# Nyström attention and a SiLU MLP on one core: a written-out order, a compact Newton-Schulz iteration, and C v by single heads

## The chip, the core and the metric

The kernel runs on one core of a Trainium2 chip. A core has five engines with a queue of instructions each: TensorE (PE: matmuls, with a second row PEld for its weight loads), VectorE (DVE), ScalarE (ACT), GpSimd (POOL) and SyncE (SP). An engine takes its instructions in the order in which they were issued, and an instruction that waits for a semaphore holds up all that stand behind it. 16 DMA engines move data; in this kernel POOL issues the loads that change type on the way (fp32 to bf16 or fp16), SP the transposes and most stores. The metric is the device time of one execution in microseconds, the lower the better. A profile is taken of one execution; its span goes from the first to the last instruction.

## The reference

Eight batches, eight heads, 576 positions, head size 64. Each sequence is cut into 32 segments; the means of q and k over a segment are the landmarks.

```python
q_lm = q.reshape(B, H, m, S // m, D).mean(axis=3)     # m = 32
k_lm = k.reshape(B, H, m, S // m, D).mean(axis=3)
A  = sm(q, k_lm)          # 576 x 32, softmax of scale * a b^T
Bm = sm(q_lm, k_lm)       # 32 x 32
C  = sm(q_lm, k)          # 32 x 576
Z = Bm.T / (norm1(Bm) * norminf(Bm) + 1e-06)
for _ in range(6):
    Z = 2 * Z - Z @ Bm @ Z                            # Newton-Schulz
attn = A @ Z @ C @ v
x = attn.transpose(0, 2, 1, 3).reshape(4608, 512)
h = x @ w_in                                          # 512 x 2048
out = (h * sigmoid(h)) @ w_out                        # 2048 x 512
```

All inputs and the output are fp32 in HBM.

## The kernel before

**Stages of a batch** (`attn(b)`). The eight heads are two groups (`g`) of four; four heads of 32 landmarks fill 128 partitions. q and k are loaded as bf16 (`load_qk`, names `ld1.b` for k, `ld0.b` for q; batch 0 in four parts, `ld10 ld11 ld00 ld01`) and v in three parts (`ldv0..2`). They are turned into `qT` by TensorE transposes for batches 0 to 2 (`tr`, copied out by `trc`) and by DMA transposes issued on SP from batch 3 on (`xt`, line 592). Landmarks come from TensorE sums (`lms`) or VectorE trees (`lra` to `lrd`, line 628), and are transposed by `ltr`. `sb` makes the 32x32 scores, `pb` to `bmx` their softmax, `A` and `C` the two wide score matrices, with exponentials `Ax` and `Cx` on ScalarE, row sums `S` on TensorE and `Ln`, `Rs`, `etn` to normalise A. C is transposed by TensorE for batches 0 and 1 (`ctm`) and by DMA after that (`ct`, line 856). `cv` multiplies it by v, `zt` joins C v and Z, and `m` folds that into w_in: M = Z C v w_in, so that layer 1 is A M.

**Newton-Schulz.** The state `st` of a group is 128 x 160: a block-diagonal 128x128 matrix of four heads (F = Z Bm) and, beside it, the four Z as 128x32 (`SW = 128 + L`). Iteration `ns` multiplies the 128x128 part by all 160 columns, and `nsd` (line 754, VectorE) forms 2 s - product. `f0` and line 736 make the first state; the last iteration does the 32 columns of Z alone.

**The MLP.** Layer 1 (`h0` to `h15` of a batch, `hx` for leftover columns) is A M in 128x512 PSUM banks, `g` and `gx` are the SiLU on ScalarE into fp16. Layer 2 works on pairs of 128-row tiles with seven products instead of eight (`p1` to `p7`, sums `ss` on VectorE, results `c..`, `u2` copied or added into `ost`, stores `os`); the first pair alone is done plainly (`o0` to `o3`, names `o0@5000.0` and so on, one for each quarter of `w_out`), since the sums of w_out (`wt`) are made meanwhile.

**The order.** Every step is an `Op` with its engine, its dependencies and a priority. `Plan.run` walks through a modelled time, takes on each engine the ready step with the lowest priority, and gives it PSUM banks (bank 7 and two others serve layer 2). It shifts priorities by the table `ORDER`, and where TensorE would stand idle in the first 45 us it puts in a filler, a matmul on zeros (`warm`, tile `zer`). A load may be issued when the load eight before it has landed (`swdge[-8]`), and loads of batch 3 and later also wait for transposes (`gate` in `later_loads`). All loads are issued on POOL, in this order: k and q of batches 0 and 1, v of batch 0, w_in by four column blocks (`wi0` to `wi3`, each in three parts), w_out in four parts (`wo0` to `wo3`), v of batch 1, k and q of batch 2, v of batch 2.

Of the kernel before, what the change touches and what calls it, by code (L numbers as in the profile page):

```python
# [18 lines left out]
ORDER = {  # L19
    "f0.0": (200.69, 0), "A.0": (-135.46, 12.93), "Ln11.0": (-57.289, 0), "etn1.0": (-31.554, 0),  # L20
    "ctm00.0": (-1364.2, 0), "wc.0": (-5319.5, 0), "mc11.0": (-629.91, 0), "tr10.1": (-42.668, 0),
    "trc15.1": (-1007.6, 0), "tr19.1": (-457.92, 0), "tr114.1": (-85.703, 0),
    "tr00.1": (-4845.1, 0), "tr09.1": (-1.1208, 0), "tr014.1": (-139.96, 0),
    "lms116.1": (413.98, 0), "lms000.1": (-607.71, 0), "lms006.1": (-83.37, 0),
    "lms010.1": (328.48, 0), "nsd00.1": (-627.38, 0), "ns10.1": (2306.7, 0),
    "nsd10.1": (-1204.8, 0), "A.1": (-266.77, 0), "Ax10.1": (-230.29, 0), "Rs1.1": (-127.11, 0),
    "Cx00.1": (-281, 0), "Cx01.1": (-181.38, 0), "Cx11.1": (-2693.4, 0), "tr014.2": (-314.54, 0),
    "bbd.2": (-120.57, 0), "nsd40.2": (175.02, 0), "h15.1": (234.98, 0), "lrd1.3": (-791.6, 0),
    "A.3": (-480.16, 0), "S00.3": (52.867, 0), "Ln01.3": (24.258, 0), "Ax11.3": (-2.2697, 0),
    "h3.2": (185.78, 0), "hx0.2": (41.862, 0), "h11.2": (452.76, 0), "hx8.2": (-6.3754, 0),  # L30
    "p5@5200.0": (-179, 0), "c12@5220.0": (-251.23, 0), "A.4": (-78.982, 0),
    "etn1.4": (1667.8, 0), "Cx11.4": (29.753, 0), "cv0.4": (-3300.5, 0),
    "p6@5340.0": (-4.9303, 0), "p7@5340.0": (-4146.8, 0), "Ax10.6": (162.02, 0),
    "ss00@5500.0": (-5226.2, 0), "p7@5700.0": (633.04, 0), "p4@5720.0": (524.17, 0),
}
# [31 lines left out]
class Plan:  # L67
# [3 lines left out]
    WARM = 45.0  # L71
# [9 lines left out]
    start_warm = 1.1  # L81
    filler = None

    def run(self):
        import heapq
        order = []
        for o in self.ops:
            o.left = len(o.deps)
            shift, o.ready = ORDER.get(o.name, (0.0, 0.0))
            o.prio += shift  # L90
            for d in {id(d): d for d, _ in o.deps}.values():
                d.users.append(o)
        cand = {e: [] for e in self.LAG}
        idle = {"PE": 1.0, "ACT": 1.0, "DVE": 0.9, "POOL": 1.3, "SP": 1.0}
        banks = [0] * 8
        table = ["exp"]
        group = [None, 0]
        pending = [False]
        groups = {}
        for o in self.ops:  # L100
            if o.group is not None:
                groups[o.group] = groups.get(o.group, 0) + 1
        tiled = [None]
        dmaq = [0.0]
        events = sorted(set(idle.values()) | {o.ready for o in self.ops})
        waiting = []

        def activate(o):
            for e, _ in o.engs:
                cand[e].append(o)  # L110

        for o in self.ops:
            if not o.left:
                activate(o)

        l1_at = set()
        l1_open = {}
        l1_seen = set()
        l2_on = [False]
        l2_open = {}  # L120
        wide = [False]

        def fit(o):
            if o.cls == "L2":
                pool = (7, 6) if wide[0] else (7, 6, 5)
                if o.pair is not None and l2_open:
                    n = sum(not banks[i] for i in pool)
                    if o.pair != next(iter(l2_open)) and (o.pair in l2_open or n < 2):
                        return None
            elif o.cls == "L1":  # L130
                room = 1 if pending[0] or group[0] is not None and group[1] > 3 else 4
                if wide[0]:
                    return None
                if len(l1_at) >= room:
                    return None
                pool = (4, 3, 2, 1, 0)
            else:
                pool = (0, 1, 2, 3, 4, 5) if l2_on[0] else (0, 1, 2, 3, 4, 5, 6)
            free = [i for i in pool if not banks[i]]
            return tuple(free[:o.psum]) if len(free) >= o.psum else None  # L140

        n = 0
        total = len(self.ops)
        while n < total:
            if not events:
                raise RuntimeError("plan stuck: " + ", ".join(
                    f"{o.name}" for e in cand for o in cand[e])[:600])
            t = heapq.heappop(events)
            while events and events[0] <= t + 1e-9:
                heapq.heappop(events)  # L150
            moved = True
            while moved:
                moved = False
                for e in ("PE", "ACT", "DVE", "POOL", "SP"):
                    if idle[e] > t + 1e-9:
                        continue
                    best, bslot, later, soon = None, None, None, None
                    if e == "PE":
                        wide[0] = any(o.psum == 4 and o.ready <= t + 1e-9 and (
                            o.opens is None or group[0] == o.opens) for o in cand[e])  # L160
                    for o in cand[e]:
                        r = o.ready + o.margin
                        if r > t + 1e-9:
                            if later is None or r < later:
                                later = r
                            if o.crit and (soon is None or r < soon):
                                soon = r
                            continue
                        rank = o.prio
                        if e == "PE" and tiled[0] and o.tiled == tiled[0]:  # L170
                            rank -= 1e5
                        if best is not None and rank >= brank:
                            continue
                        if e == "ACT" and o.table == "silu" and group[0] is not None:
                            continue
                        if e == "ACT" and o.group is not None and group[0] != o.group:
                            if o.early is not None and table[0] == "exp":
                                pass
                            elif group[0] is not None or l1_open:
                                continue  # L180
                            elif o.early is not None and any(
                                    x.done is None or x.done > t + 1e-9 for x in o.early):
                                continue
                            elif len(l1_at) > 2:
                                pending[0] = True
                                continue
                        if o.opens is not None and group[0] != o.opens and (
                                group[0] is not None or l1_open or len(l1_at) > 2):
                            if group[0] is None and not l1_open:
                                pending[0] = True  # L190
                            continue
                        s = None
                        if o.psum:
                            s = fit(o)
                            if s is None:
                                continue
                        best, bslot, brank = o, s, rank
                    if best is None:
                        if later is not None:
                            heapq.heappush(events, later)  # L200
                        if e == "PE" and not banks[7] and self.start_warm <= t < self.WARM and (
                                later is None or later > t + 0.12):
                            end = t + (0.22 if t < self.start_warm + 4.4 else 0.11)
                            order.append((self.filler, e, t, end, False))
                            idle[e] = end
                            heapq.heappush(events, end)
                            tiled[0] = None
                        continue
                    o = best
                    if soon is not None and not o.crit:  # L210
                        d = max(d2 for e2, d2 in o.engs if e2 == e)
                        if t + d > soon + 0.06:
# [3 lines left out]
                    for e2, d2 in o.engs:  # L216
                        cand[e2].remove(o)
                        if e2 == e:
                            dur = d2
# [95 lines left out]
def kernel(  # L315
# [9 lines left out]
    nc = tc.nc  # L325
# [880 lines left out]
```

## Time and profile before

| what | value |
|---|---|
| three runs, us | 247.73, 249.36, 249.66 (median 249.36) |
| span of the profiled execution | 246.7 us |
| granted TensorE clock | 1.00 in every stretch |
| ScalarE busy, 0 to 40, 40 to 220, 220 to 246.7 us | 30.3, 149.3, 4.1 us |
| VectorE busy, same stretches | 24.5, 134.6, 12.6 us |
| HBM read, written | 36.7 MB, 9.4 MB |

The page shows, in its second part, 40 slices of the span with one digit each: the busy share in tenths (9 is 90% or more).

```profile
PE   8999999999979999999999999999999999999993
DVE  2368956495869956949999879189798667066632
ACT  2597996599865999998668998966988978822200
POOL 8435733200022003200220040000000000000000
DMA  5999999999999979989899799897443003022352
```

How to read the rows that follow. A group of instructions reads "line, engine, operation, output<-inputs, shape, count | busy us, mean ns of one | idle time of the engine before them <-what ended it". Matmuls are pipelined, so the mean duration of one is longer than the distance between two; the distance is read from the timeline, whose rows begin with the start and the length in us of a run of like instructions. L394 is the helper through which all matmuls but two kinds of transposes go, so its groups are told apart by tiles.

### The profile page before, as it was taken

Reading aid. Unit: us, or ns where it says so; the run is one execution under the profiler, and the core shown is the slowest. Engines: PE = TensorE matmul, PEld = TensorE weight load, DVE = VectorE, ACT = ScalarE, POOL = GpSimd, SP = SyncE. Lnnn points to the kernel's source line nnn. Section 1 sums busy time; section 2 is a strip of 40 time slices with the busy share of each in tenths; the row PEclk is TensorE's granted clock in tenths of the full one; section 3 lists DMA queues with packets and bytes.
Section 4 is the critical chain, followed back from the end, with each engine's and each line's share of the span. In section 5 each row is a group of like instructions: output and inputs, shape, how many; then the busy total and the mean of one; then the engine's idle time right before and its main releaser. Section 6 shows DMA issues by size and latency. Waiting matters only on the chain.

```text
span 246.7 us, 7075 instructions
## 1 busy us (share of the span) xinstructions
PE 238.9 (97%) x2771; PEld 170.8 (69%) x2771; DVE 171.8 (70%) x441; ACT 183.6 (74%) x438; POOL 37.2 (15%) x63
## 2 busy tenths in 40 slices
PE   8999999999979999999999999999999999999993
PEld 6786565566767645577886655697886566688883
DVE  2368956495869956949999879189798667066632
ACT  2597996599865999998668998966988978822200
POOL 8435733200022003200220040000000000000000
PEclk9999999999999999999999999999999999999999
DMA  5999999999999979989899799897443003022352
GB/s 103 203 203 193 196 208 206 207 246 166 181 115 215 208 145 152 212 135 158 168 233 229 150 170 226 146 184 99 118 119 101 0 3 85 3 73 62 82 141 72
DMA packets 55874, 36.50 MB, mean 148 GB/s; under 512 B 36641, under 2 KB 47393, under 8 KB 55841
## 3 DMA queue, kind: packets, MB, share of 16 engines
q0 software_dynamic: 15264, 18.35, 44.6%
q1 hardware_dynamic: 39808, 16.92, 33.2%
q10 hardware_dynamic: 768, 0.79, 1.3%
q8 instruction: 21, 0.34, 0.5%
q14 instruction: 13, 0.10, 0.1%
HBM read 36.70 MB, written 9.44 MB: 187 GB/s over the span
## 4 chain that ended last, share of the span: by engine, by line
PE 83%; DMA 7%; DVE 3%; ACT 3%; SPq 1%; issue 1%; POOL 0%; DVEq 0%; POOLq 0%
PE ps L394 80%; DMA qT<-qk 4%; DMA qk<-in_q_dram 3%; PE ps L568 2%; SPq L592 1%; ACT m L404 1%; DVE red L628 1%; PE ps L844 1%; DVE st L754 1%; ACT ce L829 1%; ACT L956 1%; POOL qk L447 0%; ACT ln L794 0%; DVE etn L803 0%; DVE ss L1044 0%
## 5 line engine op out<-in xcount | busy, mean ns | idle before, releaser
L394 PE MATMUL ps<-etn,m 128*128 128x512 bf16 (+1 forms) x512 | 68.9, 286 | 0.4 <-ACT gm L956 0.4
L956 ACT ACTIVATE gm<-ps 128x512 f16<-128x512 f32 x128 | 66.1, 652 | 2.0 <-PE ps L394 1.8
L394 PEld LDWEIGHTS <-gm 128*128 128x128 f16 x512 | 48.7, 98 | 11.3 <-issue 2.4
L394 PE MATMUL ps<-w_out_sb,gm 128*128 128x256 f16 (+1 forms) x392 | 53.6, 281 | 0.0
L394 PEld LDWEIGHTS <-m 128*128 128x128 bf16 x512 | 32.0, 98 | 24.0 <-issue 1.8
L404 ACT COPY ost<-ps 128x256 f32<-128x256 f32 (+1 forms) x48 | 18.4, 383 | 37.4 <-PE ps L394 30.3
L394 PEld LDWEIGHTS <-ss 128*128 128x128 f16 x408 | 39.1, 98 | 6.6 <-issue 0.9
L1079 DVE TENSOR_TENSOR ost<-ost,ps 128x256 f32<-128x256 f32 x51 | 21.2, 416 | 20.4 <-PE ps L394 14.2
L394 PE MATMUL ps<-wt,ss 128*128 128x256 f16 x272 | 34.1, 273 | 0.0
L754 DVE SCALAR_TENSOR_TENSOR st<-st,ps 128x320 bf16<-128x320 bf16 (+3 forms) x54 | 21.4, 404 | 9.0 <-PE ps L394 7.8
L406 DVE CAST m<-ps 128x512 bf16<-128x512 f32 x31 | 20.0, 683 | 0.4 <-PE ps L394 0.2
L406 DVE COPY ost<-ps 128x256 f32<-128x256 f32 x22 | 9.3, 422 | 14.9 <-PE ps L394 14.8
L404 ACT CAST m<-ps 128x512 bf16<-128x512 f32 x33 | 17.9, 601 | 1.8 <-PE ps L394 1.7
L394 PE MATMUL ps<-w_out_sb,ss 128*128 128x256 f16 x136 | 17.6, 273 | 0.0
L453 POOL DMA_DIRECT2D qk<-in_k_dram x7 | 5.0, 714 | 82.7 <-DMA ct<-ce 41.9
L460 POOL DMA_DIRECT2D v<-in_v_dram x24 | 14.0, 591 | 14.5 <-PE ps L394 6.9
L394 PE MATMUL ps<-zer 128*128 128x256 bf16 x79 | 14.7, 310 | 1.1 <-DVE zer L487 1.1
L394 PE MATMUL ps<-wt,gm 128*128 128x256 f16 x120 | 15.5, 272 | 0.0
L394 PEld LDWEIGHTS <-st 128*128 128x128 bf16 x96 | 8.4, 97 | 9.0 <-issue 2.9
L394 PE MATMUL ps<-st 128*128 128x160 bf16 (+1 forms) x96 | 14.4, 225 | 0.2 <-DVE wsb L889 0.2
L829 ACT ACTIVATE ce<-ps 128x288 bf16<-128x288 f32 x32 | 12.8, 413 | 0.0
L784 ACT ACTIVATE et<-ps 128x288 bf16<-128x288 f32 x32 | 10.6, 423 | 2.3 <-PE ps L394 2.2
(91 smaller groups left out, 331.3 us busy)
## 6 DMA issues: line engine op xcount, KB each, us to landing
out_dram<-ost SPq DMA_DIRECT2D x128, 64.0 KB, 2.1
v<-in_v_dram POOLq DMA_DIRECT2D x24, 192.0 KB, 11.2
qk<-in_k_dram POOLq DMA_DIRECT2D x7, 576.0 KB, 7.5
qk<-in_q_dram POOLq DMA_DIRECT2D x7, 576.0 KB, 10.6
w_out_sb<-in_moe_w_out_dram POOLq DMA_DIRECT2D x4, 512.0 KB, 10.4
w_in_sb<-in_moe_w_in_dram POOLq DMA_DIRECT2D x4, 256.0 KB, 9.2
w_in_sb<-in_moe_w_in_dram POOLq DMA_DIRECT2D x8, 128.0 KB, 7.9
qk<-in_k_dram POOLq DMA_DIRECT2D x2, 288.0 KB, 4.3
```

Of the source, the lines that this page charges most:

```text
L394: nc.tensor.matmul(out=out_ap, lhsT=lhsT, rhs=rhs, start=start, stop=stop, skip_group_check=True)
L404: nc.scalar.copy(out=out, in_=in_)
L406: nc.vector.tensor_copy(out=out, in_=in_)
L453: lambda e, t=t, src=src: nc.gpsimd.dma_start(out=qk_r[b % 2][:, t].rearrange("p g j d -> p g (j d)"), in_=src[b].rearrange("(g h) (l j) d ...
L460: lambda e, a=a: nc.gpsimd.dma_start(out=v_r[b % 2][a * L:(a + 1) * L, :, :], in_=v[b].rearrange("h (l a x) d -> a l h (x d)", l=L, a=VA)[ ...
L568: nc.tensor.transpose(out=ps[:, n * 128:(n + 1) * 128], in_=qk[:, t, g, 2 * jp:2 * jp + 2, :].rearrange("p j d -> p (j d)"), identity=idb)
L592: lambda e, t=t, g=g: nc.sync.dma_start_transpose(out=qT[:, t, g], in_=qk[:, t, g].rearrange("p j d -> p (j d)")),
L754: nc.vector.scalar_tensor_tensor(out=s2[:, g0:g1, lo:SW], in0=s[:, g0:g1, lo:SW], scalar=2.0, in1=ps[:, 0:NG * SW].rearrange("p (g x) -> p ...
L784: lambda e, g=g, et=et, c=c: nc.scalar.activation(out=et[:, c], in_=bank(me["A"], 2 * g + c)[:, 0:HS], func=AF.Exp, scale=sc / J),
L829: nc.scalar.activation(out=ce[:, :, 0:VP].rearrange("p (i c) (a l) -> p c a i l", c=2, a=VA)[:, c], in_=bank(me["C"], 2 * g + c)[:, 0:HS]. ...
L956: lambda e, dc=dc, cell=cell: nc.scalar.activation(out=gm[:, dc, :], in_=bank(cell["o"]), func=AF.Silu),
L1079: nc.vector.tensor_tensor(out=out_, in0=x, in1=y, op=OP.add)
```

## The change

It does five things. **The order** is no longer computed: a table, `SEQUENCE`, lists all steps in the order in which they are issued, with the engine after a slash where there is a choice, and `*n` for n fillers on TensorE; `Plan.run` reads it and hands out PSUM banks first in, first out. Fillers go from 79 to 70. In the table's POOL order the loads stand as `ld11.0 ld00.0 ld01.0 ld0.1 ld1.1`, two parts of v of batch 0, the w_in parts mixed with the third and with v of batch 1, then q and k of batch 2, then w_out, then k of batch 3 with one part of its v, and the rest.

**Newton-Schulz** holds both F and Z as 128x32 (`SW = 2 * L`). The block-diagonal matrix that TensorE needs is made from F before each iteration by a new VectorE step `fb`, a multiplication by the mask `hmask` into a tile of 128x128 a group. `f0` has 32 instead of 128 columns.

**C v** is formed head by head: 128x32 parts of the array and 64 columns, 48 matmuls a batch, where two heads at a time took 128x64 parts and 128 columns, 24 matmuls. `wc` writes the result twice with broadcast reads.

**Half of k of batch 0** (`ld10`) is loaded in fp32 by SP (`ldk`) into the space of `gm`, and cast by ScalarE (640 columns) and VectorE (512).

**v of batch 1** stands in the middle of w_in in `LOADS`. One dependency of `hx` is added.

```diff
-ORDER = {
...
+SEQUENCE = """
+ldk ld11.0 const ident fold k0cACT k0cDVE k0 *15 lms100.0 lms106.0 tr10.0 tr15.0 trc15.0/ACT
...
+ns11.0 nsd11.0 S10.0 Ln10.0 S11.0 Ln11.0 Rs1.0 trc05.1/DVE fb20.0 fb21.0 ctm00.0 ctc00.0/DVE
...
+mc10.1/ACT mc11.1/ACT *1 m2.1 lra1.2 tr014.2 trc014.2/DVE o0@5001.0 o0@5000.0 h4.1 mc20.1/ACT
...
+os3@5721.0/ACT l1done.6 l1done.7 os0@5721.0/SP os2@5721.0/SP os1@5720.0/ACT
...
     def run(self):
...
+        for word in SEQUENCE.split():
+            if word[0] == "*":
+                order += [(self.filler, "PE", 0.0, 0.0, False)] * int(word[1:])
+                continue
+            name, _, e = word.partition("/")
+            o = named.pop(name)
...
+            if o.psum:
...
+                o.slot = tuple(free[:o.psum])
+                del free[:o.psum]
...
-    SW = 128 + L
+    SW = 2 * L
...
-    LOADS = "k1 q1 v0 w0 w1 w2 w3 o0 o1 o2 o3 v1".split()
+    LOADS = "k1 q1 v0 w0 w1 v1 w2 w3 o0 o1 o2 o3".split()
...
+    def first_load():
+        o = A("ldk", [("SP", 0.45)], lambda e: nc.sync.dma_start(
+            out=stage, in_=k[0][0:4].rearrange("h (l j) d -> (h l) (j d)", l=L)), [], -300,
+            dma=1.1, lag=1.0)
+        dst = qk_r[0][:, 1, 0].rearrange("p j d -> p (j d)")
+        parts = ((0, JA * Dh, "ACT", act_us), (JA * Dh, J * Dh, "DVE", dve_us))
...
-                w = bbd[:, g].rearrange("p a l -> p (a l)")
-                mm(ps[:, g * 128:(g + 1) * 128], w, w)
+                mm(ps[:, g * L:(g + 1) * L], bbd[:, g].rearrange("p a l -> p (a l)"), bmt[:, g])
...
+            def diag(it, o, g0=g0, g1=g1, n=n):
+                return chain(f"fb{it}{g0}", 0.07 + 0.00055 * 128 * n, lambda:
+                             nc.vector.tensor_tensor(
+                                 out=fb[it % 2][:, g0:g1],
+                                 in0=bc(sr[it % 3][:, g0:g1, 0:L], 4, 2),
+                                 in1=bc(hmask, n, 1), op=OP.mult), [o], 14.5 + 0.1 * g0)
...
-                        mm(ps[:, g * SW + lo:(g + 1) * SW], s[:, g, 0:128], s[:, g, lo:SW])
+                        mm(ps[:, g * SW + lo:(g + 1) * SW],
+                           fb[it % 2][:, g].rearrange("p a l -> p (a l)"), s[:, g, lo:SW])
...
-                        for p in range(2):
-                            h = 4 * g + 2 * p
-                            hs = slice(h, h + 2) if not g else slice(h + 1, h - 1, -1)
-                            mm(wv[64 * p:64 * p + 64, g], ct_r[g][0:VP, i, 64 * p:64 * p + 64],
-                               vs[:, hs, i * Dh:(i + 1) * Dh], start=(i == 0), stop=(i == VI - 1))
+                        for h in range(4):
+                            mm(wv[L * h:L * h + L, g], ct_r[g][0:VP, i, L * h:L * h + L],
+                               vs[:, 4 * g + h, i * Dh:(i + 1) * Dh], start=(i == 0),
+                               stop=(i == VI - 1))
```

## The prediction

> **What bounds the kernel now.** I read the page first (busy shares and the chain that ended last), then the groups with their shapes, then TensorE's timeline, and for the first 50 us the DMA issues. The page and the groups:
>
> ```profile
> span 246.7 us, 7075 instructions
> PE 238.9 (97%) x2771; PEld 170.8 (69%) x2771; DVE 171.8 (70%) x441; ACT 183.6 (74%) x438; POOL 37.2 (15%) x63
> ...
> PE 83%; DMA 7%; DVE 3%; ACT 3%; SPq 1%; issue 1%; POOL 0%; DVEq 0%; POOLq 0%
> ...
> L394 PE MATMUL ps<-zer 128*128 128x256 bf16 x79 | 14.7, 310 | 1.1 <-DVE zer L487 1.1
> L394 PE MATMUL ps<-st 128*128 128x160 bf16 x80 | 12.6, 235 | 0.2 <-DVE wsb L889 0.2
> L394 PE MATMUL ps<-v,ct 96*64 96x128 bf16 x192 | 7.1, 221 | 0.0
> ```
>
> TensorE is busy nearly throughout and holds 83% of the chain: in most of the span a microsecond less of its work is a microsecond less of time. The busy column overlaps pipelined matmuls, so I price by starts, from the timeline:
>
> ```profile
> 1.12 4.43 PE L394 MATMUL ps<-zer 128*128 128x256 bf16 x20 [1.12 <-DVE zer L487]
> 5.37 0.71 PE L394 MATMUL ps<-qk,idb 128*128 128x64 bf16 x18
> 5.91 0.67 PE L568 MATMUL ps<-idb,qk 128*128 128x128 bf16 x9
> ...
> 36.98 1.03 PE L394 MATMUL ps<-w_out_sb,gm 128*128 128x512 f16 x4
> ...
> 43.63 0.86 PE L394 MATMUL ps<-v,ct 96*64 96x128 bf16 x24
> 44.42 1.90 PE L394 MATMUL ps<-w_out_sb,gm 128*128 128x512 f16 x8
> ...
> 69.45 0.30 PE L394 MATMUL ps<-st 128*128 128x160 bf16 x2
> 69.59 0.65 PE L394 MATMUL ps<-et,hmask 128*128 128x288 bf16 x4
> ...
> 72.74 0.27 PE L394 MATMUL ps<-rs,fold 128*128 128x256 f16 x1 [1.63 <-DVE st L754]
> ```
>
> Priced so, C v takes 0.79 us a batch (43.63 to 44.42), a Newton-Schulz pair 0.14 (69.45 to 69.59), a 64-column matmul 29 ns (18 from 5.37 to 5.91). The same pricing of every TensorE group gives 223.0 us of real work in the kernel before. The rest of the 246.7 is 1.1 before the first filler, 12.8 of fillers (20 at 0.21, 59 at about 0.11 and what they wait), 3.7 to 4 of tail after TensorE, and some 6 of waits. The span falls in two: until the first product with `w_out` (36.98) the loads and the batch-0 chains set the pace and fillers plug the holes; after it TensorE runs almost without a hole.
>
> **The change part by part.**
>
> *Compact Newton-Schulz.* 80 matmuls go from 160 to 64 columns: 71 to 29 ns, 3.4 us less. The 16 of `f0` go from 128 columns (67.58 to 67.70 for two) to 32; the nearest row, `st` 128x32 at 79.99 and 80.04, gives 25 to 29 ns, so 0.45 less. On VectorE each iteration's L754 shrinks from 320 elements to 128 (between 315 ns at 160 and 218 at 64: 0.28) and a mask multiply of 128x256 comes in, priced by L710 at 0.28. One iteration alone, matmul start to VectorE start to next matmul, is 0.34 + 0.48 + 0.05 = 0.87 now (90.54 to 90.88 for the first part) and 0.26 + 0.28 + 0.28 + 0.05 = 0.87 then: nothing. By starts VectorE gains 54 masks (42 of 0.2, 12 half-size ones of 0.13: 10.0) and loses 9.4 on L754 and L736: +0.6 on 172 us. What covers it: in the written order TensorE has 0.92 to 7.3 us of other work between successive iterations of batches 1 to 7, so the chain just fits. If that cover were 0.2 short at all 35 places it would cost 7 us; I take 0 and keep +2.
>
> *C v by single heads.* Twelve steps of two 128-column matmuls side by side (56 ns a step) become twelve of four 64-column ones. The nearest row is `sb`, eight matmuls of 64x32 tiles that take 0.16 us with their tile switch (22.00 to 22.16), the four of a step 3 to 4 ns apart: side by side. At 29 ns a step I get 0.79 - 12 x 0.027 = 0.47 a batch, 2.6 us less in all. Were the steps 38 ns (the longer spacing of that row), 1.7 less.
>
> The Trainium skill, "TensorEngine Tiling (Array Packing)", Instruction Overhead, says the contrary: about 60 cycles for each matmul however short, and no tiling factor to be taken from a dimension that is already small. Charged to each of the 48, 25 ns apiece, C v would cost 1.2 us a batch, 3.3 more in all instead of 2.6 less, and the forecast would be 5.9 higher. The `sb` row speaks for one such floor per set of tiles.
>
> *Total.* 223.0 - 3.4 - 0.45 - 2.6 = 216.6 us of real work.
>
> *Written order, v of batch 1 early, and the start.* Now the last w_out part lands at 40.3, and the q of batch 2 (issued at 33.19) at 48.9; v of batch 1 lies between. The new POOL order puts v of batch 1 and both loads of batch 2 ahead of w_out. The bytes up to there are the same and the DMA share is 9 tenths throughout, so the last w_out part lands near 48.9 and the first three spacings of 2.55 earlier, at 41.3. The first `o0` can't start sooner, and everything behind it in TensorE's queue waits with it. The written order has 27.0 us of real work ahead of it, the old one 22.5 ahead of its own. So at 41.3 the kernel before has 223.0 - 22.5 - (41.3 - 36.98) = 196.2 us to go, the new one 216.6 - 27.0 = 189.6: **6.6 less**. The other three parts land 7.65 us later in all, and the order has 8.9 of work between the first users of the first and the last: no wait of its own. If the start is slower than the loads (ScalarE's and VectorE's sums up to there are about those of before), `o0` comes up to 2 later; if HWDGE's start brings all loads forward, 0.6 earlier. Nine fillers fewer change nothing here, they plug holes.
>
> *Half of k in fp32 over SP.* SP stands idle at the start and POOL drops one issue of 0.6 to 0.7 us. The transfer is the same read on the same 16 DMA engines, which are busy from 2.7 us on, so it gains what lies before that: 0 to 0.7. Two casts are added in series (640 elements on ScalarE, by the 512-element copy of 0.60 about 0.7; 512 on VectorE), so the first transposes come between 0.4 earlier and 0.6 later than 5.37. What hides it: the wait for q, which lands at 8.76 and 10.19 now. Without that cover +0.6.
>
> The Trainium skill, "TensorE: Matmul & The Clock Gate", Part 1, says that the array runs at half rate until a free-running window of about 3.4 us was busy. Here the row is the 20 fillers at 0.21 us and full pace from 5.37; with 15 fillers and a hole behind them the page would allow a slow stretch into the first transposes, about 1 us, behind the wait for q too.
>
> *Transposes by DMA.* The wait of 1.63 before 72.74 ends a chain through L592, whose first issue, at 61.14, had waited 10.3 us for a part of v. The written order loads k of batch 3 and one v part first after w_out and issues its transposes ahead of the first stores. I take 1.6 out; from 0 to 3 of the 5.5 us of waits between 36.98 and TensorE's end.
>
> *Tail.* The last copy is followed by three stores on ScalarE's queue instead of halves spread over two (2.0 against 1.7 to landing, 0.4 an issue): +0.3, bounds 0 and 0.6.
>
> **Sum.** 246.7 - 6.6 - 1.6 + 0.3 = 238.8 span. The median of the three runs, 249.36, is 2.66 above the profiled span; with that, 241.4.
>
> **The rivals.** A (0.62): as above. Its own range from the bounds (-0.6 to +2 at the start, -1.4 to +1.6 waits, +2 masks, +0.9 C v) is 239 to 246, without all upper bounds at once.
>
> B (0.13): the written order also closes the remaining 3.9 us of waits. For: the hole at 72.74 is an order's fault. Against: two independent queues rarely leave none. 237.5.
>
> C (0.15): the saving is waited out. TensorE reaches the `o0` parts no sooner, and the gaps between iterations, cut close to 0.87, open by 0.2 now and then: 241.4 + 2 (start) + 4.5 = 248.
>
> D (0.10): slower. The place is the DMA transposes: five sets of q and k for batches 3 to 7 and six of `ct` for 2 to 7, eleven in all, at which the fixed TensorE order has nothing else to put in. Against it: C to C v has 7.6 to 15 us of work, while four exponentials (0.39 each), two issues of 1.23 and 2.5 to landing make 7.2. For it: L592 transposes took up to 5.4 to land, and batch 3's cover is only 0.4. It decides from 10.5 / 11 = 0.95 us lost at each place; at 1.15 the time is 254.
>
> **How the numbers follow.** The time is A's. A measurement of this kernel can't tell 1% from no change: the bounds are 246.9 and 251.9. Faster: A nearly whole (0.60), B 0.13, half of C 0.07, together 0.80. Same: rest of A 0.02, C's other half 0.06, together 0.08. Slower: D 0.10 and a sliver of C, 0.12. The range runs from B's 237.5, less 0.5, to C's 248.5: it leaves out D and edges of B and C, under 2 in 10.
>
> **What would show it.** `v,ct` 96*32 matmuls: 48 in 0.4 to 0.5 us by starts, not 1.2. `st` pairs 0.06 apart. The first w_out matmul with 512 columns near 41, TensorE's end near 235, its idle rows between under 5 us in all. The hole at L628 gone. VectorE's busy time rises, since a short instruction's row overlaps its neighbours'. Wrong if `o0` starts after 43.5, or if idle time before `fb`-fed matmuls sums to over 3 us.

## The result, and the profile after

The kernel after takes 264.81 us (median of four runs, 263.51 to 265.19) beside 248.97 for the kernel before on the same chip (247.73 to 249.66): a ratio of 1.063, with a 95% interval of 1.058 to 1.068. The prediction of 241.4 was wrong in sign. The profiled execution has a span of 262.9 us, 24.1 more than the 238.8 of the prediction's sum. The ratios below leave out executions more than 1.5% above the fastest of the same kernel (seven of ten in experiment 1, two of four in 2, 4 and 14, one of ten in 3 and 7), while the medians and ranges below hold all of them.

The page after, first busy shares, slices, the chain that ended last, and two groups:

```profile
span 262.9 us, 7480 instructions
PE 237.3 (90%) x2954; PEld 165.0 (63%) x2954; DVE 180.4 (69%) x499; ACT 184.4 (70%) x436; POOL 36.9 (14%) x62
...
PE   7999899999899793899999990499999999999992
PEclk9999999999999898699999997599999999999998
DMA  6999999998799999702699999933141413003334
...
PE 71%; DMA 16%; DVE 4%; ACT 4%; SPq 3%; issue 1%; DVEq 0%; ACTq 0%; POOLq 0%
...
L575 DVE TENSOR_TENSOR red<-qT 128x1024 f16<-128x1024 bf16 x12 | 8.3, 688 | 19.4 <-DMA qT<-qk 19.3
...
L325 PE MATMUL ps<-rs,fold 128*128 128x256 f16 x12 | 3.5, 293 | 16.0 <-DVE rs L575 16.0
```

TensorE's share falls from 97% to 90%, and transfers hold 16% of the chain where they held 7. The slices show the place: TensorE drops to 3 tenths around 100 us and to 0 around 160, its granted clock drops to 6 and 5 tenths in the slice behind each, and the DMA engines show 9 in the slices of both. The two groups name the wait: VectorE's trees wait 19.3 us in all for DMA transposes, and `ltr` on TensorE (`rs,fold`) 16.0 for the trees. TensorE's timeline after, a few of its rows:

```profile
1.12 3.38 PE L325 MATMUL ps<-zer 128*128 128x256 bf16 x15 [1.12 <-DVE zer L434]
4.98 0.51 PE L325 MATMUL ps<-qk,idb 128*128 128x64 bf16 x12 [0.47 <-ACT qk L335]
...
42.06 1.89 PE L325 MATMUL ps<-w_out_sb,gm 128*128 128x512 f16 x8
...
71.40 0.28 PE L325 MATMUL ps<-rs,fold 128*128 128x256 f16 x1 [1.15 <-DVE rs L575]
71.61 0.55 PE L325 MATMUL ps<-v,ct 96*32 96x64 bf16 x48
...
80.92 0.23 PE L325 MATMUL ps<-st,fb 128*128 128x64 bf16 x2
80.99 0.59 PE L325 MATMUL ps<-etn,m 128*128 128x512 bf16 x2
...
89.47 0.60 PE L325 MATMUL ps<-v,ct 96*32 96x64 bf16 x48 [1.92 <-DMA ct<-ce]
...
105.98 0.37 PE L325 MATMUL ps<-rs,fold 128*128 128x256 f16 x1 [4.87 <-DVE rs L575]
...
168.27 0.40 PE L325 MATMUL ps<-rs,fold 128*128 128x256 f16 x1 [10.02 <-DVE rs L575]
```

The parts that the prediction priced by starts are there: C v takes 0.49 us a batch, a Newton-Schulz pair 0.07 (80.92 to 80.99), the first product with `w_out` starts at 42.06. What was not forecast stands in the brackets: stops of 1.92, 4.87 and 10.02 us, beside the one of 1.63 that shrank to 1.15.

The chain of waits after, in order of time (start, length, what), leads each long stop back to one transpose:

```profile
91.44 12.12 DMA qT<-qk
103.64 0.70 DVE red L575
104.37 0.44 DVE red L575
105.22 0.42 issue
105.64 0.29 DVE rs L575
105.98 7.61 PE ps L325 x47
...
151.75 14.10 DMA qT<-qk
165.93 0.70 DVE red L575
166.66 0.43 DVE red L575
167.41 0.60 DVE ss L1001
168.27 90.05 PE ps L325 x1015
```

These are the last transposes of batches 4 and 6, which took 12.12 and 14.10 us; the longest of the 32 DMA transposes before took 5.38. For the line that issues those of q and k, first before, then after:

```profile
DMA to landing us min/median/max: 3.2/3.4/5.4
...
DMA to landing us min/median/max: 3.2/4.8/14.1
```

Why they were slow is read from the issues on SP and POOL from 84 to 105 us, first after (start, length of the run of issues, engine, line), then before:

```profile
85.92 7.87 SPq L539 DMA_TRANSPOSE qT<-qk  x4
...
91.12 0.71 POOL L400 DMA_DIRECT2D qk<-in_k_dram  x1 [15.60 <-DMA qT<-qk]
91.82 0.59 POOL L407 DMA_DIRECT2D v<-in_v_dram  x1
92.41 0.72 POOL L400 DMA_DIRECT2D qk<-in_q_dram  x1
```

```profile
88.98 6.53 SPq L592 DMA_TRANSPOSE qT<-qk  x4
...
96.83 0.71 POOL L453 DMA_DIRECT2D qk<-in_k_dram  x1 [19.98 <-DMA qT<-qk]
97.53 0.71 POOL L453 DMA_DIRECT2D qk<-in_q_dram  x1
```

Before, the loads of batch 5 begin at 96.83, when three transposes of batch 4 have landed and the fourth, issued at 94.2, is 0.7 us from it. After, they begin at 91.12, a moment ahead of the issue of the fourth (91.44), with one landed. The second and third, issued ahead of the same loads (88.54 and 89.95), still land in 5.0 and 4.5 us; only the one issued behind them takes 12.12. In batch 6 it is the same: the two issued ahead of the loads land in 3.4 and 3.3, the last, issued behind the first four of seven, in 14.10. The gate that keeps them apart is in `later_loads`, and the change did not touch it:

```python
gate = last[b - 1].get("xts", [])[-2:-1]
...
load_qk(b, 100.0 * b - 150, p["qk_read"], gate)
```

The list holds xt10, xt11, xt00 and xt01, so the slice is `xt00` alone. It stands for "nearly all transposes have landed" only while `xt00` is issued third. The written SP order has `xt00.4 xt01.4 xt10.4 xt11.4` and `xt00.6 xt10.6 xt11.6 ... xt01.6`: the gate opens on the first of four.

### The profile page after: what moved, and what is told of

The parts are those of the page before. It is cut to its first block, busy times and chain, and to the rows that moved or that the text cites. A ratio compares the mean times of both kernels' runs of the same rounds, so it can differ in the third digit from the quotient of the medians.

```text
span 262.9 us, 7480 instructions
## 1 busy us (share of the span) xinstructions
PE 237.3 (90%) x2954; PEld 165.0 (63%) x2954; DVE 180.4 (69%) x499; ACT 184.4 (70%) x436; POOL 36.9 (14%) x62
## 4 chain that ended last, share of the span: by engine, by line
PE 71%; DMA 16%; DVE 4%; ACT 4%; SPq 3%; issue 1%; DVEq 0%; ACTq 0%; POOLq 0%
PE ps L325 68%; DMA qT<-qk 11%; DMA qk<-in_k_dram 2%; DMA out_dram<-ost 2%; PE ps L515 2%; SPq L539 2%; ACT gm L913 2%; DVE red L575 2%; SPq L978 1%; ACT ce L787 1%; PE ps L802 1%; DVE ss L1001 0%; ACT L1116 0%; DVE ost L1036 0%; DVE rs L575 0%
## 5 line engine op out<-in xcount | busy, mean ns | idle before, releaser
L913 ACT ACTIVATE gm<-ps 128x512 f16<-128x512 f32 x128 | 69.5, 632 | 15.3 <-PE ps L325 15.1
L325 PE MATMUL ps<-etn,m 128*128 128x512 bf16 (+1 forms) x512 | 76.6, 297 | 0.0
L325 PEld LDWEIGHTS <-m 128*128 128x128 bf16 x512 | 32.2, 100 | 28.8 <-issue 12.1
L335 ACT CAST m<-ps 128x512 bf16<-128x512 f32 x39 | 21.0, 602 | 3.3 <-PE ps L325 3.2
L575 DVE TENSOR_TENSOR red<-qT 128x1024 f16<-128x1024 bf16 x12 | 8.3, 688 | 19.4 <-DMA qT<-qk 19.3
L710 DVE SCALAR_TENSOR_TENSOR st<-st,ps 128x128 bf16<-128x128 bf16 (+2 forms) x54 | 13.7, 259 | 8.4 <-PE ps L325 7.8
L337 DVE CAST m<-ps 128x512 bf16<-128x512 f32 x25 | 16.4, 684 | 3.0 <-PE ps L325 2.8
L337 DVE COPY ost<-ps 128x256 f32<-128x256 f32 (+1 forms) x27 | 11.5, 430 | 9.9 <-PE ps L325 6.7
L325 PE MATMUL ps<-rs,fold 128*128 128x256 f16 x12 | 3.5, 293 | 16.0 <-DVE rs L575 16.0
L752 ACT ACTIVATE ln<-ps 128x288 f32<-128x288 f32 x32 | 12.3, 422 | 4.4 <-PE ps L325 4.4
L685 DVE TENSOR_TENSOR fb<-st,hmask 128x256 bf16<-128x256 bf16 (+1 forms) x54 | 14.3, 274 | 1.3
## 6 DMA issues: line engine op xcount, KB each, us to landing
w_out_sb<-in_moe_w_out_dram POOLq DMA_DIRECT2D x4, 512.0 KB, 14.1
```

The source lines that it names most:

```text
L325: nc.tensor.matmul(out=out_ap, lhsT=lhsT, rhs=rhs, start=start, stop=stop, skip_group_check=True)
L335: nc.scalar.copy(out=out, in_=in_)
L337: nc.vector.tensor_copy(out=out, in_=in_)
L575: lambda e: nc.vector.tensor_tensor(out=o_, in0=a_, in1=b_, op=OP.add),
L685: nc.vector.tensor_tensor(out=fb[it % 2][:, g0:g1], in0=bc(sr[it % 3][:, g0:g1, 0:L], 4, 2), in1=bc(hmask, n, 1), op=OP.mult), [o], 14.5 + ...
L710: nc.vector.scalar_tensor_tensor(out=s2[:, g0:g1, lo:SW], in0=s[:, g0:g1, lo:SW], scalar=2.0, in1=ps[:, 0:NG * SW].rearrange("p (g x) -> p ...
```

## The experiments

**1. The transposes of batches 4 and 6 in their old order, nothing else.**

```diff
-wrc.3 nsd20.3 xt00.4
+wrc.3 nsd20.3 xt10.4
...
-g13.3 xt01.4 xt10.4 xt11.4
+g13.3 xt11.4 xt00.4 xt01.4
...
-ct0.5 xt00.6
+ct0.5 xt10.6 xt11.6 xt00.6 xt01.6
...
-ldv0.6 xt10.6 xt11.6 os@5301.0
+ldv0.6 os@5301.0
...
-lrc1.6 xt01.6 lrd1.6
+lrc1.6 lrd1.6
```

> The kernel after, with nothing changed but the place of the four DMA transposes of q and k in the written SP order of batches 4 and 6: xt10, xt11, xt00, xt01 one behind the other, instead of xt00 first. Theory G (the gate is defeated): the loads of batch b+1 wait for one transpose only, xt00 of batch b; issued first it opens them while the other three are still to come, so these ran among the loads and took 12.1 and 14.1 us to land (91.44 and 151.75 in the trace after), TensorE stopped for 4.9 and 10.0 us and its clock fell to half. G expects the last transpose of batches 4 and 6 to land within 6 us of its issue, the two stops at 106 and 168 under 1.5 us each and the half-clock stretches gone: about 265 - 15 - 3 = 247, between 241 and 252. Rival L (the written queues are late as a whole, whichever transpose is first): transposes still over 8 us, time above 258. Rival S (the fixed TensorE order has no slack, any lateness is lost): the stops move to the next place, 254 to 262.

Measured: 251.31 us (median of ten, 246.99 to 253.96); by the three executions that the ratio holds 0.998 of the kernel before (0.994 to 1.002), so about 248. The last transposes of batches 4 and 6 land 3.9 and 3.3 us after their issue, and the two long stops are gone. TensorE's timeline, the rows with a wait of over 1 us, from an execution of 251.49:

```profile
88.68 0.56 PE L325 MATMUL ps<-v,ct 96*32 96x64 bf16 x48 [1.58 <-DMA ct<-ce]
...
110.66 0.43 PE L325 MATMUL ps<-qT,lmT 64*32 64x288 bf16 x15 [1.33 <-DVE ost L1036]
...
166.87 0.23 PE L325 MATMUL ps<-st,fb 128*128 128x64 bf16 x2 [3.60 <-DVE fb L685]
```

G holds for the 16 us: eight words of the order, and no matmul, vector step or transfer more or less. G did not name the stop of 3.60, which in this execution has a half-clock stretch of 3.41 us behind it. What stays is smaller stops, and a time equal to that of before by the ratio and 1.1% above it by the medians of all (248.49 before), not 7 us below it. No run moves the gate and leaves the order alone. That it is the loads that make the transposes late rests on the traces: in all of them, every transpose that took over 6 us was issued with loads under way.

**2. The reverse: in the kernel before, `xt00` is issued first in batches 4 and 6.**

```diff
     order = P.run()
+    for u in (4, 6):
+        at = {o.name: i for i, (o, *_) in enumerate(order) if o.name[:2] == "xt"}
+        i, j, k = (at[f"xt{x}.{u}"] for x in ("10", "11", "00"))
+        first, second, third = order[i], order[j], order[k]
+        order[i], order[j], order[k] = third, first, second
```

> The kernel before, with xt00 moved ahead of the other three DMA transposes in batches 4 and 6 of its finished order and nothing else. Theory G (loads open on xt00 alone): the loads of batches 5 and 7 start among the transposes here too, these take over 8 us to land, and the time goes from 249 to between 252 and 262. Rival L (lateness comes from the written POOL and SP order): transposes land in 3 to 5.5 us as before, time 248 to 250. Rival S (the order of before has slack for late transposes): they land late but the time stays within 248 to 251.

Measured: 265.54 us (median of four, 260.75 to 272.06), 1.049 (1.043 to 1.055), so about 261. The chain of waits, from an execution of 269.87, has the same two steps in a kernel with none of the rest of the change:

```profile
92.75 13.47 DMA qT<-qk
...
108.29 36.07 PE ps L394 x396
...
151.15 14.31 DMA qT<-qk
...
165.58 0.70 DVE red L628
...
168.37 95.91 PE ps L394 x990
```

So neither lateness of the written queues (L) nor a lack of slack peculiar to the written TensorE order is needed: the order of before loses 12 us to the same slip.

**3 and 4. The first experiment with one compact part undone.** The third has C v by pairs of heads again, the fourth the 160-column Newton-Schulz without `fb`.

> The kernel of the first experiment (transposes in the order 10, 11, 00, 01) with C v back as pairs of heads: 24 matmuls of 96x64 by 128 columns a batch instead of 48 of 96x32 by 64. Prediction's price (side by side, 0.79 us a batch against 0.49): 2.4 to 2.6 us slower than the first experiment. Rival (TensorE waits elsewhere at those places, so the work is no bound): 0 to 1 slower. Against both, a fixed cost for each matmul would make it 1 to 3 faster.

> The kernel of the first experiment with Newton-Schulz back as it was: iterates stored as 128 block-diagonal columns plus 32, matmuls of 160 columns, no mask step on VectorE, f0 of 128 columns. Prediction's price: 3.8 us slower than the first experiment. Rival M (the mask step that the compact form adds on VectorE lies in the chain from iteration to iteration and eats the gain): 0 to 1 slower, or faster; then short holes ahead of matmuls fed by fb in the first experiment's trace should sum to over 2 us and be gone here.

Measured: 250.00 us (247.04 to 253.17; 1.002, 0.998 to 1.006) and 251.41 (248.22 to 253.82, four runs, no ratio), beside 251.31 for the first. By the ratios the old C v costs 0.9 us with about 1.5 either way, which leaves room for nothing and, at its edge, for the price of 2.4; by the medians of all ten it is 1.3 faster. The two lowest of the old Newton-Schulz lie 0.6 above the three lowest of the first experiment (means of 248.88 and 248.25), far from 3.8, with too few executions to say more. By starts TensorE does spend less in the compact forms (C v 3.90 us in all instead of 6.34, `ns` 2.89 instead of 5.78), so the work is saved. The hole of 3.60 ahead of a matmul fed by `fb` is not the sign that rival M named, many short ones: at the same place the third, with `fb` too, waits 1.09 and the fourth, without it, 0.58. What ate the saving these two do not show.

**5 and 6. The compact parts in the kernel before**, whose own order is kept step by step: the fifth with C v by single heads, the sixth with both (a mask step issued directly behind the VectorE step that feeds it).

> The kernel before with C v by single heads (48 matmuls of 96x32 by 64 columns a batch) and nothing else: its finished order of all operations is the same, operation by operation. Prediction's price (P): TensorE is the bound there, 2.6 us less in all, 2.3 of it after the first product with w_out: 246 to 247 beside 248.5. Rival W (transfers set the pace of the batches, so less TensorE work only waits): 248 to 249, and TensorE's idle time grows by the 2.3.

> The kernel before with C v by single heads and the compact Newton-Schulz, again in its own finished order (each mask step directly behind the VectorE step that feeds it). P: 6.4 us of TensorE work less, 5 to 5.5 of it after the first product with w_out, so 243 to 244.5 beside 248.5. W: 246.5 to 249, TensorE's idle time 3 us or more above the 4.0 of before. If the mask step lies on the chain: idle time ahead of the matmuls fed by fb over 2 us.

Measured: 248.14 us (1.000, 0.997 to 1.003) and 248.40 (1.001, 0.998 to 1.004). Neither reaches what P needs, though by starts, waits taken off, C v goes from 6.49 to 4.12 us in the fifth, and `ns` in the sixth from 6.11 to 3.61. TensorE's idle time is 3.8 in the fifth and 7.7 in the sixth, beside 4.0. W expected that of the sixth, but not of the fifth, whose profiled execution was 1.6 us shorter than that of before: between 0 and the 0.8 that its interval allows, its gain stays open. Nor does the sixth's trace, of an execution of 250.05, give W's reason: behind the first product with `w_out` all its waits are put down to VectorE and ScalarE, none to a transfer, and ahead of the matmuls fed by `fb` it waits 2.2 us, over the 2 that was set as the sign for a mask step on the chain (1.3 of it put down to `wsb`, 0.3 to `fb`).

**7. Two more slips mended in the written order** of the first experiment.

```diff
-ld0.5 xt01.5 ldv2.4 os@5120.0
+ld0.5 xt00.5 xt01.5 ldv2.4 os@5120.0
...
-l1done.2 xt00.5
+l1done.2
...
-xt11.7 xt01.7 xt10.7 xt00.7
+xt10.7 xt11.7 xt00.7 xt01.7
```

> The kernel of the first experiment with two more places of the SP order mended: xt00 of batch 5 goes with the other three, ahead of a batch of stores, and the four of batch 7 come in the order 10, 11, 00, 01, which is the order in which VectorE's trees use them. The stops of 1.3 us at 110.7 and of 1.1 to 3.6 us at 163 to 167 should go. If these slips of the written order hold what the compact parts save (theory G, continued): 2 to 4 us less than the first experiment's 248, so 244 to 246. If the transfers as a whole set the pace (W): the waits come back elsewhere, 247 to 249.

Measured: 248.03 us, 1.000 (0.996 to 1.005): the continued G misses, W has it. The stop at 110.7 shrinks to 0.16, and there are waits beside it, 2.8 us each on `ct` of batch 3 and on `fb` behind the trees of batch 7. The trace is of the longest of the ten executions, 251.62; the third's, at 247.04, has 1.54 and 1.09 at these places.

**8 to 10. Less to transfer.** Of v for batches 4 to 7 only the first head of each part is loaded (so C v of those batches uses old values in the rest): in the kernel before, in the sixth kernel, in the seventh.

```diff
-                out=v_r[b % 2][a * L:(a + 1) * L, :, :],
+                out=v_r[b % 2][a * L:(a + 1) * L, 0:H if b < 4 else 1, :],
```

> The kernel before with seven eighths of the loads of v left out for batches 4 to 7 (of each of the three parts only the first head is loaded, the rest of the tile keeps older values; order and instructions as before). It shortens the stream of loads and transposes by up to 3 us a batch and leaves TensorE's work alone. If TensorE is the bound (P): only its waits between 60 and 170, about 1 us, can go: 247 to 248.5. If the stream of transfers paces the batches (W) and TensorE's 97% is a coincidence of the two: still no more than those waits, 246 to 248.5; this run is the base for the next one.

> The kernel before with C v by single heads and compact Newton-Schulz, in its own order, and with the same seven eighths of v's loads of batches 4 to 7 left out. W: with the stream shorter the saved TensorE work (5 to 5.5 us) shows at last, 4 to 6 us below the run before it: 242 to 244.5. If the waits come from the mask steps and the order on VectorE, and not from transfers (V): 246.5 to 249, as with all loads.

> The kernel with the tidied written order (transposes of batches 4 to 7 mended) and the same part of v's loads left out. W: the waits on ct at 89 (2.8 us) and behind the trees at 167 (2.8 us) shrink to under 1 us each and the time falls to 241 to 245, near the 241.4 of the prediction. V, or a loss at the start of the written order: 246 to 249.

Measured: 248.33 us (0.998, 0.995 to 1.001); 247.40 (0.996, 0.995 to 0.998); 244.08 (0.984, 0.981 to 0.986). With fewer bytes the kernel before stays where it was, and the written order gains 4 us. In the tenth the wait on `ct` of batch 3 is 0.1 and that on `fb` is gone; of the stops after the first product with `w_out` this is left:

```profile
71.87 0.28 PE L322 MATMUL ps<-rs,fold 128*128 128x256 f16 x1 [1.01 <-DVE pbs L837]
...
109.08 0.43 PE L322 MATMUL ps<-qT,lmT 64*32 64x288 bf16 x15 [0.29 <-DVE ost L1034]
...
111.79 1.03 PE L322 MATMUL ps<-wt,gm 128*128 128x256 f16 x8 [0.49 <-DVE ost L1034]
...
155.67 1.06 PE L322 MATMUL ps<-etn,m 128*128 128x512 bf16 x18 [0.41 <-ACT gm L911]
```

So W is right for the written order and V's time for the order of before, where the compact parts gain only 0.4 (by the ratios) to 0.9 (by the medians) even with fewer bytes. That the tenth's gain is the saved work is read from TensorE's sum beside the eighth: without fillers all matmuls take 6.4 us less by starts, fillers 0.9 less, idle time is 2.2 more, and its last matmul ends 5.1 sooner (238.1 and 243.2). No run has the old parts in the written order with fewer bytes. In the ninth the same sum is 4.8 less work, 0.3 more in fillers and 3.1 more idle time, 2.1 of it ahead of the first product with `w_out`. One group of the ninth holds 2.0 of its waits:

```profile
L395 PE MATMUL ps<-st,fb 128*128 128x64 bf16 x80 | 9.7, 195 | 2.0 <-DVE wsb L902 1.3 <-DVE fb L739 0.4
```

There the matmuls fed by mask steps wait for VectorE, 1.3 us of it put down to the step `wsb` and 0.4 to the mask step itself; in the kernel after, whose written order puts other matmuls between, this group waits 0.0.

**11 and 12. The same bytes in other places.** The eleventh is the seventh with part 0 of v of batch 4 moved into the next lot of loads and parts 0 and 2 of batch 7 behind its last transpose; the twelfth loads parts 0 and 2 of batch 3 earlier as well.

```diff
-ldv0.2 ct0.2 ld0.4
+ldv0.2 ldv0.3 ldv2.3 ct0.2 ld0.4
...
-cv0.3 ldv0.4
+cv0.3
...
-ld0.5 xt00.5 xt01.5
+ld0.5 ldv0.4 xt00.5 xt01.5
...
-xt10.7 xt11.7 xt00.7 xt01.7
+xt10.7 xt11.7 xt00.7 xt01.7 ldv0.7 ldv2.7
...
+    for x in (0, 2):
+        v_ops[B - 1][x].after = last[B - 1]["xts"][-1:]
```

> The tidied written order (transposes of batches 4 to 7 mended), with all loads, and three parts of v moved out of the lots of loads that the late transposes shared: v part 0 of batch 4 from the lot of batch 4 to that of batch 5, parts 0 and 2 of batch 7 behind the last transpose of batch 7. If the contention of loads and transposes holds what is left (W, from the run with less v: 244.1 beside 248.0): ct of batch 3 lands about 1 us sooner, xt of batch 7 about 2, the waits at 89 and 167 fall from 2.8 each to about 1.8 and under 1, and the time to 245 to 246.5. If it was the amount of data and not its place: 247.5 to 249.

> The run before, with parts 0 and 2 of v of batch 3 loaded ahead of the lot of batch 4 too, right behind the loads of batch 2 and 3. ct of batch 3 then shares its time with less: it lands 2 us sooner and its wait at 89 goes (1.8 less). Against it, these two parts fall on the transposes of batch 3, whose wait at 70 may grow by up to 2. W: 243.5 to 246; if the two cancel, the same as the run before it.

Measured: 247.19 us (0.994, 0.990 to 0.999) and 246.17 (0.989, 0.986 to 0.993). The twelfth is 1.1% faster than the kernel before and computes all of the reference. Both times miss W's ranges from above, the eleventh's by 0.7 and the twelfth's by 0.2, though the waits that were to go went: in the eleventh that on `ct` is 1.00 and that at 167 is gone, in the twelfth both are. In the eleventh a stop of 2.9 us at 111 came in: the first `xt` of batch 5, which now shares with the part that moved, takes 7.5 us to land where the seventh's took 6.0. The same stop, 2.28 us, is the longest that the twelfth keeps:

```profile
66.35 1.03 PE L322 MATMUL ps<-w_out_sb,gm 128*128 128x256 f16 x8 [0.82 <-DVE ost L1033]
...
110.87 0.43 PE L322 MATMUL ps<-qT,lmT 64*32 64x288 bf16 x15 [2.28 <-DVE ost L1033]
```

**13 and 14. The kernel after with one batch mended**: the thirteenth batch 4, the fourteenth batch 6.

> The kernel after with the order 10, 11, 00, 01 of the transposes in batch 4 alone; in batch 6 xt00 stays first. If the losses add by place, with those of the trace (10.0 us of stop ahead of the trees' sums of batch 6, some 1.7 by the half clock behind it): 248 + 11.5 = 259.5, between 257 and 262. If one late place takes up what the other lost (the later one only because TensorE came early): 264, as with both.

> The kernel after with the four transposes of batch 6 together in the order 10, 11, 00, 01; in batch 4 xt00 stays first. If the losses add by place (4.9 of stop at batch 5, some 2.2 by the half clock behind it, less the 2 of wait that the mended order has there itself): 248 + 5 = 253, between 251.5 and 255.5. If the delay is made up before the end: 248 to 250.

Measured: 257.56 us (1.037, 1.032 to 1.042) and 256.89 (253.84 to 258.57, no ratio), beside 248.46. Left as it was, batch 6 alone costs 9.6 over the first experiment's 248.0, less than the 11.5 expected but inside its range. Batch 4 alone costs 7.0 by its two lowest executions (253.84 and 256.12), more than the 5 expected, in part since its stop is 6.91 us here and not 4.87:

```profile
105.18 0.37 PE L322 MATMUL ps<-rs,fold 128*128 128x256 f16 x1 [6.91 <-DVE rs L572]
```

Together 16.6, beside 16.1 with both: the two places add up, though the 7.0 rests on two executions.

## Why the prediction was wrong, step by step

*What bounds the kernel now: "a microsecond less of its work is a microsecond less of time".* This step failed, and with it the 6.6 us. The work did fall about as priced: C v by 2.6 us in all (forecast 2.6), `ns` by 3.3 (3.4), `f0` by 0.5 (0.45). But in the order of before 2.4 and then 5.3 us less by starts moved the time by less than 1 (experiments 5 and 6), and in the written order, its gate mended, the time was that of before (experiment 1). A TensorE at 97% says that its queue was full, not that nothing else runs as close to the end. In the written order that was the stream of loads and transposes up to 166 us (with fewer bytes 4 us went, 10). In the order of before it stays open: fewer bytes gave nothing there (8), waits for VectorE grew with the mask steps (6, 9), and the fifth kernel has no mask steps and gains no more than 0.8.

*"Transposes by DMA."* This is the step that set the sign. It read the SP order for what stood behind what on SP, and took a stop of 1.6 us out. It did not ask what waits for `xt00`. The hole did shrink, to 1.15, while two transposes that land in 3 to 5.5 us in the kernel before took 12 and 14. The first and second experiment show that the place of `xt00` alone makes the 16 us in the kernel after, and 12 in the kernel before.

*Rival D* had the right place, the transposes, and the right reason for the loss, that the fixed TensorE order has nothing else to put in. Its price had the wrong form: 1.15 us at each of eleven places, where two places cost 9.6 and 7.0. The bound from the nearest rows, "up to 5.4 to land", came from a trace in which the gate kept loads and transposes apart, and the change undid just that. Rival C's 248 is where the kernel lands with the gate mended (1); that is partly luck, since C saw the saving lost to a start 2 us late and to many short gaps between iterations. The start came 0.9 late (42.20), and the waits are a few long ones, behind transposes and VectorE's trees.

*The sum by terms.* Of the 24.1 us between forecast and profile, 0.8 lies ahead of the first product with `w_out` (42.06, forecast 41.3), 0.6 in the tail, and 22.8 between. Of these the stops make 14.4 (18.3 less the 3.9 allowed). Half pace makes some 5.6: an estimate from the granted clock, 0.50 during 11.2 us of work behind the stops. The remaining 2.8 stands in no wait that the profile shows. It may be a matter of counting: of the 5.5 us of waits that the prediction found by subtraction in the kernel before, the idle rows show 2.2. No run separates the clock from the stops.

*What held.* The start came within its bounds, and neither of the prediction's own signs of being wrong was seen (`o0` after 43.5, over 3 us of idle time ahead of `fb`-fed matmuls). The slow stretch that it allowed for behind 15 fillers did not come either: the granted clock is 1.00 from 4.50 us on, and the first transposes start at 4.98. The mask steps cost nothing in the kernel after, and VectorE's busy time rose (171.8 to 180.4) as foreseen. The charge of some 60 cycles for every small matmul, which the Trainium skill has in "TensorEngine Tiling (Array Packing)", Instruction Overhead, is not seen: 48 matmuls on 96x32 parts take 0.49 us, 10 ns each, where by the prediction's estimate the charge would give 1.2 us.

## What to carry to other kernels

When an order is rewritten, list every wait that names one member of a set as a stand-in for all, and look at where that member stands in the new order: a gate on one of four transposes is only as good as its being late. Before a microsecond of the busiest engine is counted as one of time, look for the second-closest chain; here 6.4 us of saved TensorE work showed as 4, and that only in the order that covers the mask steps, and with fewer bytes to load. A bound taken from rows of a profile holds only while what keeps those rows apart stays in force.

## What the runs showed of the hardware

A DMA transpose that is issued behind loads lands about when the loads do; one issued a little ahead of them is not held up (5.0 and 4.5 us in batch 4 of the kernel after). The 2.5 to 5.4 us from issue to landing of the kernel before become 12.1 and 14.1 with four and seven loads under way (13.5 and 14.3 in the second experiment, with five); the loads of the first case were issued from 91.12 on and landed by 103.16, the transpose at 103.56. The page "DMA: Bandwidth & Descriptors", Rules for kernel authors, in the Trainium skill says that a transpose next to ordinary DMAs needs nothing; that is said of correct data, and for the time these runs show otherwise.

The granted clock fell to half at some stops of 1.9 us and more, in stretches of 3.41, 6.83 and 10.24 us, one, two and three times the same length: in the kernel after 3.41 behind the stop of 1.9, 6.83 and 10.24 beginning in those of 4.9 and 10.0. Stops of 1.5 and 1.6 (experiments 3 and 1) and one of 2.1 and one of 2.6 (14) brought none, one of 2.3 (12) did. The Trainium skill, "TensorE: Matmul & The Clock Gate", Part 1, gives a free-running window of 3413 ns; the lengths agree with it.
